# A fixed order for the head of the kernel, a conversion on three engines, and weights from a free place

## Chip, cores, metric

One core of a Trainium2 chip. The metric is the device time of one execution in microseconds (us), lower is better. The engines go by the profile's names: PE is TensorE (matmuls; PEld its weight loads), DVE is VectorE, ACT is ScalarE, POOL is GpSimd, SP is SyncE; ACTq and SPq are the DMA issues of ACT and SP. TensorE is called warm where its matmuls run at full clock and cold where they take about twice as long.

## The reference

```
x   (8, 3008, 256) float32          w_in (256, 2048), w_out (2048, 256) float64
X = real(fft(fft(x, axis=1), axis=2))      # FNet mixing
h = X.reshape(24064, 256) @ w_in
out = maximum(0.01 * h, h) @ w_out
```

The product of a float32 array and a float64 scalar makes both weights float64, so the kernel gets them as pairs of 32-bit words and has to build float32 from them.

## The kernel before

Each sequence is folded, transformed along the sequence by matmuls ("dft"), and the transform along the features is folded into the first weights ("weight fold", `wf`). The body has 384 steps, each an "up" (first product, leaky relu) and, three steps later, a "down" (second product). All of that is one TensorE stream. Feature d=128 has a path of its own: "nyquist", a broadcast `nb`, and weights `wn`. The parts that matter here, cut to their core:

```python
def g_tile():                                     # raw pieces, scratch and the steps' g share 5 buffers
    return work.tile([P, 2 * WN], F32, tag="g", bufs=5, name="raw")

def to_f32(dst, raw, dtype):                      # 512 float64 a partition, all on DVE
    ...
    v.tensor_scalar(man_i, hi, 0xFFFFF, 0x100000, and, or)                          # L240
    v.scalar_tensor_tensor(man, lo * 2.0**-32 + man_i)                              # L241
    v.tensor_scalar(power_i, (hi >> 20) & 0x7FF)                                    # L242
    v.tensor_scalar(power_i, min(max(power_i, 896), 1151))                          # L243
    v.tensor_scalar(power_i, (power_i - 896) * 2**23)                               # L244
    v.scalar_tensor_tensor(power_i, (hi & sign) | power_i)                          # L245
    v.scalar_tensor_tensor(dst, (man * 2.0**-20) * power)                           # L246

def w_in_part(f0):                                # two pieces, tag "win", 2 buffers
    ...
    for w in range(2):                            # weight fold: cosine, sine
        ... matmul(pt, lhsT=feat_sb[:, a, w * P : (w + 1) * P], rhs=win[a]); scalar.copy(wf[...], pt)
    for i in range(4):                            # L265: weights of d=128, one column each
        ... matmul(pt[:, i : i + 1], lhsT=win[a][:, i * P : (i + 1) * P], rhs=feat_sb[:, a, 2 * P : 2 * P + 1])
    nc.scalar.copy(wn[...], pt[:, 0:4])

load_x(0); fold_x(0); load_tab(nc.scalar, ...)    # the scheduler may reorder each engine's work
for f0 in range(0, F, WN): w_in_part(f0)
nyquist(0); dft(units[0], 0); dft(units[0], 1); spread(units[0])
for f in range(0, NH, 2): w_out_part(f)
nyquist(1)
for at in range(len(steps) + lag): up(at); ...; down(at - 3)
```

Of the kernel before, what the change touches and what calls it, by code (L numbers as in the profile page):

```python
# [47 lines left out]
P = 128  # L49
# [10 lines left out]
WN = 512  # L60
SLOPE = 0.01
# [46 lines left out]
def feat_tables():  # L108

    j, d = np.arange(D)[:, None], np.arange(P)[None, :]  # L110
    turn = (j * d) % D
    cos = np.where(4 * turn % (2 * D) == D, 0.0, np.cos(2.0 * np.pi * turn / D))
    sin = np.where(2 * turn % D == 0, 0.0, np.sin(2.0 * np.pi * turn / D))
    nyq = np.where(j % 2 == 0, 1.0, -1.0)
    out = np.zeros((D, 2 * P + 2), np.float32)
    out[:, 0:P] = cos
    out[:, P : 2 * P] = -sin
    out[:, 2 * P :] = nyq
    return out
# [29 lines left out]
def tile_fnet_leaky_relu(  # L149
# [24 lines left out]
    xs = {}  # L174

    def load_x(b):
        t = xp.tile([P, 2, 2, NI * 2, D], F32, tag="x", bufs=1, name="xt")
        for h in range(2):
            nc.sync.dma_start(t[:, h], x[b, :, h].rearrange("p e i r d -> p e (i r) d"))
        xs[b] = t  # L180
# [3 lines left out]
    def fold_x(b):  # L184


        t = xs.pop(b)
        a, z = t[:, :, 0], t[:, :, 1]
        nc.vector.tensor_tensor(a, a, z, op=ALU.add)  # L189
        for h in range(2):  # L190
            lo, hi = a[:, h, :, 1:P], a[:, h, :, P + 1 : D]
            nc.vector.tensor_tensor(z[:, h, :, 1:P], lo, hi, op=ALU.add)
            nc.vector.tensor_tensor(z[:, h, :, P + 1 : D], lo, hi, op=ALU.subtract)
            nc.scalar.copy(z[:, h, :, 0:1], a[:, h, :, 0:1])
            nc.gpsimd.memset(z[:, h, :, P : P + 1], 0.0)
# [5 lines left out]
    feat_sb = const.tile([P, 2, 2 * P + 2], F32, name="feat_sb")  # L201
    nc.sync.dma_start(feat_sb, feat_tab.rearrange("(a p) n -> p a n", p=P))
    load_x(0)
# [4 lines left out]
    nyx = const.tile([P, 2, 2, NI, 2, B], F32, name="nyx")  # L208
    tabs = {}
# [6 lines left out]
    def g_tile():  # L216
        return work.tile([P, 2 * WN], F32, tag="g", bufs=5, name="raw")

    def load_w(src):

        raw = g_tile()
        n = src.shape[1] * src.shape[2]
        dst = raw if src.dtype == F32 else raw.bitcast(src.dtype)
        nc.sync.dma_start(dst[:, 0:n].rearrange("p (c n) -> p c n", c=src.shape[1]), src)
        return raw

    def to_f32(dst, raw, dtype):
# [3 lines left out]
        if dtype == F32:  # L231
            nc.vector.tensor_copy(dst, raw[:, 0:WN])
            return
        hi = raw.bitcast(I32)[:, 0 : 2 * WN].rearrange("p (n w) -> p n w", w=2)[:, :, 1]
        lo = raw.bitcast(U32)[:, 0 : 2 * WN].rearrange("p (n w) -> p n w", w=2)[:, :, 0]
        tmp = g_tile()
        man, power = tmp[:, 0:WN], tmp[:, WN : 2 * WN]
        man_i, power_i = tmp.bitcast(I32)[:, 0:WN], tmp.bitcast(I32)[:, WN : 2 * WN]
        v = nc.vector
        v.tensor_scalar(man_i, in0=hi, scalar1=0xFFFFF, scalar2=0x100000, op0=ALU.bitwise_and, op1=ALU.bitwise_or)  # L240
        v.scalar_tensor_tensor(man, in0=lo, scalar=2.0**-32, in1=man_i, op0=ALU.mult, op1=ALU.add)  # L241
        v.tensor_scalar(power_i, in0=hi, scalar1=20, scalar2=0x7FF, op0=ALU.logical_shift_right, op1=ALU.bitwise_and)  # L242
        v.tensor_scalar(power_i, in0=power_i, scalar1=896.0, scalar2=1151.0, op0=ALU.max, op1=ALU.min)  # L243
        v.tensor_scalar(power_i, in0=power_i, scalar1=-896.0, scalar2=2.0**23, op0=ALU.add, op1=ALU.mult)  # L244
        v.scalar_tensor_tensor(power_i, in0=hi, scalar=-(2**31), in1=power_i, op0=ALU.bitwise_and, op1=ALU.bitwise_or)  # L245
# [206 lines left out]
```

## Time and profile before

| | |
|---|---|
| time, median | 2002.47 us (2002.25 to 2003.03); 2002.72 in the rounds of the change |
| span of the profiled run | 1999.3 us |
| first matmul | 31.29 us |
| TensorE uninterrupted from | 97.47 us |
| one step from then on | 4.66 us |

The prediction below shows the lines. Read them so: TensorE is full from 97 us to the end, so only what happens before that can move the time, and that stretch ("the head") is where DVE is nearly always busy.

### The profile page before, as it was taken

To read this page: it belongs to the slowest core of one execution; us is meant where nothing else is said; L and a number is where in the kernel's file an instruction comes from. 1 tells how busy PE (TensorE), PEld (TensorE's weight loads), DVE (VectorE), ACT (ScalarE), POOL (GpSimd) and SP (SyncE) were. 2 spreads that over 40 slices of the span, in tenths; PEclk is the share of its full clock that TensorE was granted. 3 is DMA by queue.
4 is the path that set the end of the run, shared out by engine and by line. 5 is a ranking of instruction groups with operands and counts; after the bars stand their busy time and mean duration, and the time that the engine had idled before them with its cause. 6 is when DMAs were issued, how large, how long until landed. Compare 5 with 4: busy or idle time off the path is not lost.

```text
span 1999.3 us, 24452 instructions
## 1 busy us (share of the span) xinstructions
PE 1950.6 (98%) x8952; PEld 1691.1 (85%) x8952; DVE 1106.4 (55%) x2111; ACT 439.1 (22%) x496; POOL 1095.0 (55%) x1572
## 2 busy tenths in 40 slices
PE   3799999999999999999999999999999999999999
PEld 1488888888888888888888888888888888888888
DVE  6945654466454744557445475545644475455444
ACT  0122222222222222222222222222222222222221
POOL 0365755566455655556555475555655566455554
PEclk9899999999999999999999999999999999999999
DMA  6301000020000200002000100002000020000000
GB/s 247 101 11 74 19 21 19 11 82 22 11 19 11 92 11 19 11 22 82 11 19 21 74 19 11 29 11 82 14 18 19 11 82 21 11 19 17 16 11 21
DMA packets 23478, 70.98 MB, mean 36 GB/s; under 512 B 2480, under 2 KB 15152, under 8 KB 21312
## 3 DMA queue, kind: packets, MB, share of 16 engines
q1 hardware_dynamic: 22208, 64.80, 8.9%
q10 hardware_dynamic: 1152, 4.63, 0.6%
q8 instruction: 71, 1.16, 0.2%
q14 instruction: 47, 0.39, 0.1%
HBM read 44.71 MB, written 24.71 MB: 35 GB/s over the span
## 4 chain that ended last, share of the span: by engine, by line
PE 96%; DVE 2%; DMA 1%; issue 0%; SPq 0%; DVEq 0%
PE sum_ps L380 57%; PE sin_ps L347 16%; PE cos_ps L347 16%; PE dft_ps L291 6%; PE up_ps L260 1%; DMA xt<-in_x_dram 1%; PE up_ps L265 0%; DVE raw L240 0%; DVE raw L241 0%; DVE raw L245 0%; DVE raw L244 0%; DVE raw L243 0%; DVE xt L189 0%; DVE win L246 0%; DVE wo L246 0%; DVE raw L242 0%
## 5 line engine op out<-in xcount | busy, mean ns | idle before, releaser
L352 DVE SCALAR_TENSOR_TENSOR cos<-nb,wn,cos_ps 128x251 f32<-128x251 f32 (+1 forms) x768 | 330.9, 472 | 731.0 <-PE cos_ps L347 731.0
L362 POOL TENSOR_TENSOR s<-g 128x251 f32<-128x251 f32 (+1 forms) x384 | 294.5, 767 | 783.7 <-ACT g L358 783.7
L358 ACT ACTIVATE g<-g 128x1004 f32<-128x1004 f32 (+1 forms) x384 | 399.1, 1039 | 1347.0 <-DVE g L357 1292.3
L380 PE MATMUL sum_ps<-s,wt 128*128 128x251 f32 (+1 forms) x2304 | 550.3, 374 | 0.0
L380 PEld LDWEIGHTS sum_ps<-s,wt 128*128 128x128 f32 x2304 | 434.2, 188 | 54.5
L347 PE MATMUL sin_ps<-mix,wf 128*128 128x251 f32 (+1 forms) x1536 | 390.6, 376 | 8.7 <-DVE nyq L300 4.8
L347 PE MATMUL cos_ps<-mix,wf 128*128 128x251 f32 (+1 forms) x1536 | 389.7, 376 | 2.0 <-DVE cos L352 2.0
L380 PE MATMUL sum_ps<-g,wo 128*128 128x251 f32 (+1 forms) x1536 | 388.6, 375 | 0.0
L347 PEld LDWEIGHTS sin_ps<-mix,wf 128*128 128x128 f32 x1536 | 291.8, 190 | 44.7 <-DVE nyq L300 5.2
L380 PEld LDWEIGHTS sum_ps<-g,wo 128*128 128x128 f32 x1536 | 291.9, 190 | 40.8
L347 PEld LDWEIGHTS cos_ps<-mix,wf 128*128 128x128 f32 x1536 | 292.3, 190 | 37.2 <-DVE cos L352 2.7
L365 POOL TENSOR_TENSOR s<-g,s 128x251 f32<-128x251 f32 (+1 forms) x384 | 275.1, 716 | 30.1
L363 POOL TENSOR_TENSOR s<-s,g 128x251 f32<-128x251 f32 (+1 forms) x384 | 291.4, 759 | 0.0
L356 DVE TENSOR_TENSOR g<-cos,sin_ps 128x502 f32<-128x502 f32 (+1 forms) x384 | 260.1, 677 | 50.5 <-DVE cos L352 10.5
L357 DVE TENSOR_TENSOR g<-cos,sin_ps 128x502 f32<-128x502 f32 (+1 forms) x384 | 257.4, 670 | 0.0
L364 POOL TENSOR_TENSOR s<-g 128x251 f32<-128x251 f32 (+1 forms) x384 | 253.0, 659 | 0.0
L380 PE MATMUL sum_ps<-s,wo 128*128 128x251 f32 (+1 forms) x768 | 225.2, 375 | 0.0
L380 PE MATMUL sum_ps<-g,wt 128*128 128x251 f32 (+1 forms) x768 | 225.2, 375 | 0.0
L380 PEld LDWEIGHTS sum_ps<-s,wo 128*128 128x128 f32 x768 | 145.6, 190 | 17.0
L380 PEld LDWEIGHTS sum_ps<-g,wt 128*128 128x128 f32 x768 | 145.9, 190 | 16.5
L291 PE MATMUL dft_ps<-tab,xt 128*128 128x377 f32 (+1 forms) x384 | 126.7, 479 | 0.0
L291 PEld LDWEIGHTS dft_ps<-tab,xt 128*128 128x128 f32 x384 | 72.6, 189 | 43.0 <-issue 0.6
(42 smaller groups left out, 434.3 us busy)
## 6 DMA issues: line engine op xcount, KB each, us to landing
xt<-in_x_dram SPq DMA_DIRECT2D x16, 1536.0 KB, 6.5
out_dram<-o SPq DMA_DIRECT2D x80, 251.0 KB, 2.3
tab<-in_seq_tab_dram ACTq DMA_DIRECT2D x8, 565.5 KB, 11.8
raw<-in_w_in_dram SPq DMA_DIRECT2D x8, 512.0 KB, 4.0
raw<-in_w_out_dram SPq DMA_DIRECT2D x8, 512.0 KB, 3.7
out_dram<-o SPq DMA_DIRECT2D x16, 250.0 KB, 2.1
nb<-nyq_dram SPq DMA_DIRECT2D x8, 376.5 KB, 3.5
nb<-nyq_dram SPq DMA_DIRECT2D x8, 376.0 KB
```

What stands on the lines that cost most here:

```text
L260: nc.tensor.matmul(pt, lhsT=feat_sb[:, a, w * P : (w + 1) * P], rhs=win[a], start=(a == 0), stop=(a == 1))
L291: nc.tensor.matmul(ps_t[0:m, 0 : KW[c]], lhsT=z_of(i), rhs=tabs[n, c][:, i, 0 : KW[c]], start=(i == 0), stop=(i == NI - 1))
L347: nc.tensor.matmul(pt[blk][:, h * n : (h + 1) * n], lhsT=wf[:, blk, fs], rhs=mixed[b, c][blk][:, at : at + n], start=True, stop=True)
L352: nc.vector.scalar_tensor_tensor(cos[:, hs], in0=spreads[b, c][:, at : at + n], scalar=wn[:, h * NH + f : h * NH + f + 1], in1=pt[0][:, hs ...
L356: nc.vector.tensor_tensor(g[:, 0], cos[:, 0 : 2 * n], pt[1][:, 0 : 2 * n], op=ALU.add)
L357: nc.vector.tensor_tensor(g[:, 1], cos[:, 0 : 2 * n], pt[1][:, 0 : 2 * n], op=ALU.subtract)
L358: nc.scalar.activation(g, g, ACT.Lrelu)
L362: nc.gpsimd.tensor_tensor(s1, a[1][0], a[1][1], op=ALU.add)
L363: nc.gpsimd.tensor_tensor(s2, s1, a[0][0], op=ALU.subtract)
L364: nc.gpsimd.tensor_tensor(s3, a[0][0], a[1][0], op=ALU.subtract)
L365: nc.gpsimd.tensor_tensor(s4, a[0][1], s2, op=ALU.subtract)
L380: nc.tensor.matmul(sums[j][p], lhsT=still[p], rhs=moving[p], start=(f == 0 and i % 2 == 0), stop=(f == NH - 1), skip_group_check=True)
```

## The change

Its intent: start the TensorE stream earlier by taking float64 work off DVE, taking the one-column matmuls away, and laying the head out by hand. Its core (cuts marked):

```diff
-    out[:, 2 * P :] = nyq
+    out[:, P : P + 1] = nyq          # the sine of d=0 is zero: its column carries d=128's weights
 ...
-        v.tensor_scalar(power_i, ... max 896, min 1151)
-        v.tensor_scalar(power_i, ... -896, * 2**23)
-        v.scalar_tensor_tensor(dst, (man * 2**-20) * power)
+        nc.scalar.activation(man, man_i, ACT.Copy, scale=2.0**-20)
+        nc.scalar.activation(power, power_i, ACT.Relu, scale=-1.0, bias=inf[:, 0:1])
+        nc.scalar.activation(power_i, power, ACT.Relu, scale=-(2.0**23), bias=inf[:, 1:2])
+        nc.gpsimd.tensor_tensor(man, man, power, op=ALU.mult)
 ...
-        ... 16 one-column matmuls a part, scalar.copy(wn)
+        nc.scalar.dma_start(wn_dram row, wf[0:1, 1] ...)      # spread_wn: out and in again through DRAM
+        nc.scalar.dma_start(wn[...], row ...)
 ...
-    raw pieces and scratch in g (5 buffers), win 2 buffers
+    raw pieces in tags o, e, raw (5 buffers), power 2, win 4
 ...
+    with tc.manual_schedule():        # every engine keeps this order
+        w0 = load_w_in(0); t0 = load_x(0, nc.scalar); nc.scalar.dma_start(nyx); feat_sb; w2 = load_w_in(2 * WN)
+        load_tab(nc.scalar, 0..3, 0); o0 = load_w_out(0)
+        w0.begin; w0.end; fold_rows(t0, 0, nc.gpsimd); fold_w_in(0, w0); w1 = load; w2.begin
+        fold_rows(t0, 1, nc.gpsimd); w2.end; fold_halves; fold_nyquist; rest = nyquist(0); fold_w_in(2 * WN, w2)
+        wn_rest = spread_wn(0); o0.begin; rest(); spread; wn_rest(); w3 = load; rest = dft(0); o0.end; combine; rest()
+        rest = dft(1); w1.begin; rest(); step(0); w1.end; fold_w_in(WN, w1); step(1); w3.begin; step(2); w3.end
+        fold_w_in(3 * WN, w3); wn_rest = spread_wn(WN); step(3); o1.begin; wn_rest(); step(4); o1.end; combine; o2.begin
+        step(5); o2.end; combine; o3.begin; step(6); o3.end; combine; load_tab(nc.sync, 0..3, 1); step(7); step(8)
+        nyquist(1)(); spread(units[1])
+    for at in range(9, len(steps) + lag): step(at)
```

`begin` is the part of a conversion up to the activations, `end` what follows them.

More of the change, by code (lines that the diff above doesn't have):

```diff
@@ L60 @@
 WN = 512
+WB = WN // D
 SLOPE = 0.01
@@ L114, in feat_tables @@
     nyq = np.where(j % 2 == 0, 1.0, -1.0)
-    out = np.zeros((D, 2 * P + 2), np.float32)
+    out = np.zeros((D, 2 * P), np.float32)
     out[:, 0:P] = cos
     out[:, P : 2 * P] = -sin
-    out[:, 2 * P :] = nyq
+    out[:, P : P + 1] = nyq
     return out
@@ L172, in dft_ps, with load_x, fold_rows, fold_halves @@
         return up_ps("dft_ps")
-    xs = {}
-    def load_x(b):
+    def load_x(b, q=None):
         t = xp.tile([P, 2, 2, NI * 2, D], F32, tag="x", bufs=1, name="xt")
         for h in range(2):
-            nc.sync.dma_start(t[:, h], x[b, :, h].rearrange("p e i r d -> p e (i r) d"))
-        xs[b] = t
+            (q or nc.sync).dma_start(t[:, h], x[b, :, h].rearrange("p e i r d -> p e (i r) d"))
+        return t
     zs = {}
-    def fold_x(b):
-        t = xs.pop(b)
-        a, z = t[:, :, 0], t[:, :, 1]
-        nc.vector.tensor_tensor(a, a, z, op=ALU.add)
-        for h in range(2):
-            lo, hi = a[:, h, :, 1:P], a[:, h, :, P + 1 : D]
-            nc.vector.tensor_tensor(z[:, h, :, 1:P], lo, hi, op=ALU.add)
-            nc.vector.tensor_tensor(z[:, h, :, P + 1 : D], lo, hi, op=ALU.subtract)
-            nc.scalar.copy(z[:, h, :, 0:1], a[:, h, :, 0:1])
-            nc.gpsimd.memset(z[:, h, :, P : P + 1], 0.0)
+    def fold_rows(t, h, minus):
+        a, z = t[:, h, 0], t[:, h, 1]
+        nc.vector.tensor_tensor(a, a, z, op=ALU.add)
+        lo, hi = a[:, :, 1:P], a[:, :, P + 1 : D]
+        minus.tensor_tensor(z[:, :, P + 1 : D], lo, hi, op=ALU.subtract)
+        nc.vector.tensor_tensor(z[:, :, 1:P], lo, hi, op=ALU.add)
+        nc.scalar.copy(z[:, :, 0:1], a[:, :, 0:1])
+        nc.gpsimd.memset(z[:, :, P : P + 1], 0.0)
+    def fold_halves(b, t):
+        a, z = t[:, :, 0], t[:, :, 1]
         nc.vector.tensor_tensor(a[:, 0], z[:, 0], z[:, 1], op=ALU.add)
@@ L198, in fold_x @@
         zs[b] = a
-    feat_sb = const.tile([P, 2, 2 * P + 2], F32, name="feat_sb")
-    nc.sync.dma_start(feat_sb, feat_tab.rearrange("(a p) n -> p a n", p=P))
-    load_x(0)
+    feat_sb = const.tile([P, 2, 2 * P], F32, name="feat_sb")
     wf = const.tile([P, 2, F], F32, name="wf")
@@ L208, in tile_fnet_leaky_relu @@
     nyx = const.tile([P, 2, 2, NI, 2, B], F32, name="nyx")
+    inf = const.tile([P, 2], F32, name="inf")
+    wn_dram = dram.tile([2, F // 2], F32, name="wn_dram")
     tabs = {}
@@ L214, in load_tab @@
         tabs[n, c] = t
-    def g_tile():
-        return work.tile([P, 2 * WN], F32, tag="g", bufs=5, name="raw")
-    def load_w(src):
-        raw = g_tile()
-        n = src.shape[1] * src.shape[2]
-        dst = raw if src.dtype == F32 else raw.bitcast(src.dtype)
-        nc.sync.dma_start(dst[:, 0:n].rearrange("p (c n) -> p c n", c=src.shape[1]), src)
-        return raw
-    def to_f32(dst, raw, dtype):
-        if dtype == F32:
-            nc.vector.tensor_copy(dst, raw[:, 0:WN])
-            return
-        hi = raw.bitcast(I32)[:, 0 : 2 * WN].rearrange("p (n w) -> p n w", w=2)[:, :, 1]
-        lo = raw.bitcast(U32)[:, 0 : 2 * WN].rearrange("p (n w) -> p n w", w=2)[:, :, 0]
-        tmp = g_tile()
-        man, power = tmp[:, 0:WN], tmp[:, WN : 2 * WN]
-        man_i, power_i = tmp.bitcast(I32)[:, 0:WN], tmp.bitcast(I32)[:, WN : 2 * WN]
-        v = nc.vector
-        v.tensor_scalar(man_i, in0=hi, scalar1=0xFFFFF, scalar2=0x100000, op0=ALU.bitwise_and, op1=ALU.bitwise_or)
-        v.scalar_tensor_tensor(man, in0=lo, scalar=2.0**-32, in1=man_i, op0=ALU.mult, op1=ALU.add)
-        v.tensor_scalar(power_i, in0=hi, scalar1=20, scalar2=0x7FF, op0=ALU.logical_shift_right, op1=ALU.bitwise_and)
-        v.tensor_scalar(power_i, in0=power_i, scalar1=896.0, scalar2=1151.0, op0=ALU.max, op1=ALU.min)
-        v.tensor_scalar(power_i, in0=power_i, scalar1=-896.0, scalar2=2.0**23, op0=ALU.add, op1=ALU.mult)
-        v.scalar_tensor_tensor(power_i, in0=hi, scalar=-(2**31), in1=power_i, op0=ALU.bitwise_and, op1=ALU.bitwise_or)
-        v.scalar_tensor_tensor(dst, in0=man, scalar=2.0**-20, in1=power, op0=ALU.mult, op1=ALU.mult)
@@ L248, in w_in_part, with __init__, word, begin @@
-    def w_in_part(f0):
-        n = w_in.shape[1] // F
-        win = []
-        for a in range(2):
-            raw = load_w(w_in[a * P : (a + 1) * P, n * f0 : n * (f0 + WN)].rearrange("p (c n) -> p c n", c=1))
-            w = work.tile([P, WN], F32, tag="win", bufs=2, name="win")
-            to_f32(w, raw, w_in.dtype)
-            win.append(w)
+    class Weights:
+        def __init__(self, src, dst):
+            n = len(parts)
+            tag, bufs = (("o", 2), ("e", 2), ("raw", 1))[n % 3]
+            self.raw = work.tile([P, 2 * WN], F32, tag=tag, bufs=bufs, name="raw")
+            self.dst = dst
+            self.f64 = src.dtype != F32
+            raw = self.raw if not self.f64 else self.raw.bitcast(src.dtype)
+            nc.sync.dma_start(raw[:, 0 : src.shape[1] * src.shape[2]].rearrange("p (c n) -> p c n", c=src.shape[1]), src)
+            parts.append(self)
+        def word(self, dtype, w):
+            return self.raw.bitcast(dtype).rearrange("p (n w) -> p n w", w=2)[:, :, w]
+        def begin(self):
+            if not self.f64:
+                return
+            hi = self.word(I32, 1)
+            self.power = work.tile([P, WN], F32, tag="power", bufs=2, name="power")
+            man, power = self.dst, self.power
+            man_i, power_i = man.bitcast(I32), power.bitcast(I32)
+            v = nc.vector
+            v.tensor_scalar(man_i, in0=hi, scalar1=0xFFFFF, scalar2=0x100000, op0=ALU.bitwise_and, op1=ALU.bitwise_or)
+            v.tensor_scalar(power_i, in0=hi, scalar1=20, scalar2=0x7FF, op0=ALU.logical_shift_right, op1=ALU.bitwise_and)
+            nc.scalar.activation(man, man_i, ACT.Copy, scale=2.0**-20)
+            nc.scalar.activation(power, power_i, ACT.Relu, scale=-1.0, bias=inf[:, 0:1])
+            nc.scalar.activation(power_i, power, ACT.Relu, scale=-(2.0**23), bias=inf[:, 1:2])
+        def end(self):
+            if not self.f64:
+                nc.vector.tensor_copy(self.dst, self.raw[:, 0:WN])
+                return
+            hi, lo = self.word(I32, 1), self.word(U32, 0)
+            man, power = self.dst, self.power
+            power_i = power.bitcast(I32)
+            v = nc.vector
+            v.scalar_tensor_tensor(man, in0=lo, scalar=2.0**-52, in1=man, op0=ALU.mult, op1=ALU.add)
+            v.scalar_tensor_tensor(power_i, in0=hi, scalar=-(2**31), in1=power_i, op0=ALU.bitwise_and, op1=ALU.bitwise_or)
+            nc.gpsimd.tensor_tensor(man, man, power, op=ALU.mult)
@@ L257, in w_in_part, with load_w_in, fold_w_in @@
+    parts = []
+    def load_w_in(f0):
+        n, made = w_in.shape[1] // F, []
+        for a in range(2):
+            w = work.tile([P, WN], F32, tag="win", bufs=4, name="win")
+            src = w_in[a * P : (a + 1) * P, n * f0 : n * (f0 + WN)].rearrange("p (c n) -> p c n", c=1)
+            made.append(Weights(src, w))
+        return made
+    def fold_w_in(f0, made):
         for w in range(2):
@@ L259, in w_in_part, with spread_wn, rest, load_w_out @@
             for a in range(2):
-                nc.tensor.matmul(pt, lhsT=feat_sb[:, a, w * P : (w + 1) * P], rhs=win[a], start=(a == 0), stop=(a == 1))
+                nc.tensor.matmul(pt, lhsT=feat_sb[:, a, w * P : (w + 1) * P], rhs=made[a].dst, start=(a == 0), stop=(a == 1))
             nc.scalar.copy(wf[:, w, f0 : f0 + WN], pt)
-        pt = up_ps()
-        for i in range(WN // P):
-            for a in range(2):
-                nc.tensor.matmul(pt[:, i : i + 1], lhsT=win[a][:, i * P : (i + 1) * P],
-                                 rhs=feat_sb[:, a, 2 * P : 2 * P + 1], start=(a == 0), stop=(a == 1))
-        nc.scalar.copy(wn[:, f0 // P : f0 // P + WN // P], pt[:, 0 : WN // P])
-    def w_out_part(f):
-        nf = WN // D
+    def spread_wn(f0):
+        row = wn_dram[:, f0 : f0 + WN]
+        nc.scalar.dma_start(row.rearrange("(o h) n -> o h n", o=1), wf[0:1, 1].rearrange("o (h n) -> o h n", h=2)[:, :, f0 : f0 + WN])
+        at = f0 // P
+        def rest():
+            for h in range(2):
+                nc.scalar.dma_start(wn[:, h * NH + at : h * NH + at + WN // P], row[h].rearrange("(q p) -> p q", p=P))
+        return rest
+    def load_w_out(f):
+        made = []
         for h in range(2):
             at = (h * NH + f) * P
-            raw = load_w(w_out[at : at + nf * P, :].rearrange("(c p) d -> p c d", p=P))
-            to_f32(wo[:, h, f : f + nf, :].rearrange("p c d -> p (c d)"), raw, w_out.dtype)
-        b = [[wo[:, h, f : f + nf, i * P : (i + 1) * P] for i in range(2)] for h in range(2)]
-        t = [wt[:, i, f : f + nf, :] for i in range(4)]
+            src = w_out[at : at + WB * P, :].rearrange("(c p) d -> p c d", p=P)
+            made.append(Weights(src, wo[:, h, f : f + WB, :].rearrange("p c d -> p (c d)")))
+        return made
+    def combine_w_out(f):
+        b = [[wo[:, h, f : f + WB, i * P : (i + 1) * P] for i in range(2)] for h in range(2)]
+        t = [wt[:, i, f : f + WB, :] for i in range(4)]
         for to, x, y in ((t[0], b[0][1], b[0][0]), (t[1], b[1][1], t[0]), (t[2], b[1][1], b[0][1]), (t[3], b[1][0], t[1])):
             nc.gpsimd.tensor_tensor(to, x, y, op=ALU.subtract)
-    fold_x(0)
-    for n in range(4):
-        load_tab(nc.scalar, n, 0)
-    for f0 in range(0, F, WN):
-        w_in_part(f0)
-    nc.sync.dma_start(nyx, x_nyq)
     def sequence(ps_t, m, z_of, n, c):
@@ L305, in dft @@
         z = zs[b]
-        t = work.tile([P, UW[0]], F32, tag=f"mix{blk}", bufs=2, name=f"mix{blk}")
         pe, po = dft_ps(), dft_ps()
@@ L309, in dft, with rest, fold_nyquist @@
             sequence(pt, P, lambda i: z[:, (c + blk) % 2, 2 * i + r, blk * P : (blk + 1) * P], 2 * blk + r, c)
-        butterfly(t, pe, po, P, c)
-        mixed.setdefault(u, {})[blk] = t
+        def rest():
+            t = work.tile([P, UW[0]], F32, tag=f"mix{blk}", bufs=2, name=f"mix{blk}")
+            butterfly(t, pe, po, P, c)
+            mixed.setdefault(u, {})[blk] = t
+        return rest
+    nyq_dram = dram.tile([B, 2, UW[0]], F32, name="nyq_dram")
     nya, nyb = nyx[:, :, 0], nyx[:, :, 1]
-    nc.vector.tensor_tensor(nyb, nya, nyb, op=ALU.add)
-    nc.vector.tensor_tensor(nya[:, 0], nyb[:, 0], nyb[:, 1], op=ALU.add)
-    nc.vector.tensor_tensor(nya[:, 1], nyb[:, 0], nyb[:, 1], op=ALU.subtract)
-    nyq_dram = dram.tile([B, 2, UW[0]], F32, name="nyq_dram")
+    def fold_nyquist():
+        nc.vector.tensor_tensor(nyb, nya, nyb, op=ALU.add)
+        nc.vector.tensor_tensor(nya[:, 0], nyb[:, 0], nyb[:, 1], op=ALU.add)
+        nc.vector.tensor_tensor(nya[:, 1], nyb[:, 0], nyb[:, 1], op=ALU.subtract)
     def nyquist(c):
@@ L323, in nyquist, with rest @@
             sequence(pt, B, lambda i: nya[:, c, i, r, :], r, c)
-        t = work.tile([P, UW[0]], F32, tag="mix0", bufs=2, name="nyq")
-        butterfly(t, pe, po, B, c)
-        nc.sync.dma_start(nyq_dram[:, c, 0 : UW[c]], t[0:B, 0 : UW[c]])
+        def rest():
+            t = work.tile([P, UW[0]], F32, tag="mix0", bufs=2, name="nyq")
+            butterfly(t, pe, po, B, c)
+            nc.sync.dma_start(nyq_dram[:, c, 0 : UW[c]], t[0:B, 0 : UW[c]])
+        return rest
     def spread(u):
@@ L384, in down @@
         p1, p2, p3, p4, p5, p6, p7 = (sums[j][p] for p in range(7))
-        o = work.tile([P, 2, 2 * CW], F32, tag="o", bufs=2, name="o")
-        e = work.tile([P, 4, CW], F32, tag="e", bufs=2, name="e")
+        o = work.tile([P, 2 * WN], F32, tag="o", bufs=2, name="o")[:, 0 : 4 * CW].rearrange("p (a n) -> p a n", a=2)
+        e = work.tile([P, 2 * WN], F32, tag="e", bufs=2, name="e")[:, 0 : 4 * CW].rearrange("p (a n) -> p a n", a=4)
         q1, u2, u3, v = (e[:, i, 0:n] for i in range(4))
@@ L393, in down, with step @@
             nc.sync.dma_start(out[d * P : (d + 1) * P, first : first + 2 * n], o[:, d, 0 : 2 * n])
-    nyquist(0)
-    dft(units[0], 0)
-    dft(units[0], 1)
-    spread(units[0])
-    for n in range(4):
-        load_tab(nc.scalar, n, 1)
-    for f in range(0, NH, WN // D):
-        w_out_part(f)
-    nyquist(1)
     lag = 3
-    for at in range(len(steps) + lag):
+    def step(at):
         if at < len(steps):
@@ L411, in tile_fnet_leaky_relu @@
             if n + 1 < len(units) and f == 4:
+                if part == 0 and n > 0:
+                    spread(units[n + 1])
                 if part == 0:
-                    spread(units[n + 1])
                     if c == 1:
-                        fold_x(b + 1)
+                        t = xs.pop(b + 1)
+                        for h in range(2):
+                            fold_rows(t, h, nc.vector)
+                        fold_halves(b + 1, t)
                 else:
-                    dft(units[n + 1], part - 1)
+                    dft(units[n + 1], part - 1)()
@@ L418, in tile_fnet_leaky_relu @@
             if c == 0 and part == 2 and f == 6 and b + 1 < B:
-                load_x(b + 1)
+                xs[b + 1] = load_x(b + 1)
         if at >= lag:
             down(*steps[at - lag])
+    xs = {}
+    with tc.manual_schedule():
+        nc.vector.memset(inf[:, 0:1], 1151.0)
+        nc.vector.memset(inf[:, 1:2], 255.0 * 2.0**23)
+        w0 = load_w_in(0)
+        t0 = load_x(0, nc.scalar)
+        nc.scalar.dma_start(nyx, x_nyq)
+        nc.sync.dma_start(feat_sb, feat_tab.rearrange("(a p) n -> p a n", p=P))
+        w2 = load_w_in(2 * WN)
+        for n in range(4):
+            load_tab(nc.scalar, n, 0)
+        o0 = load_w_out(0)[:]
+        for w in w0:
+            w.begin()
+        for w in w0:
+            w.end()
+        fold_rows(t0, 0, nc.gpsimd)
+        fold_w_in(0, w0)
+        w1 = load_w_in(WN)
+        for w in w2:
+            w.begin()
+        fold_rows(t0, 1, nc.gpsimd)
+        for w in w2:
+            w.end()
+        fold_halves(0, t0)
+        fold_nyquist()
+        rest = nyquist(0)
+        fold_w_in(2 * WN, w2)
+        wn_rest = spread_wn(0)
+        for w in o0:
+            w.begin()
+        rest()
+        spread(units[0])
+        wn_rest()
+        w3 = load_w_in(3 * WN)
+        rest = dft(units[0], 0)
+        for w in o0:
+            w.end()
+        combine_w_out(0)
+        o1 = load_w_out(WB)
+        rest()
+        rest = dft(units[0], 1)
+        for w in w1:
+            w.begin()
+        rest()
+        step(0)
+        for w in w1:
+            w.end()
+        fold_w_in(WN, w1)
+        step(1)
+        for w in w3:
+            w.begin()
+        step(2)
+        for w in w3:
+            w.end()
+        fold_w_in(3 * WN, w3)
+        wn_rest = spread_wn(WN)
+        o2 = load_w_out(2 * WB)
+        step(3)
+        for w in o1:
+            w.begin()
+        wn_rest()
+        step(4)
+        for w in o1:
+            w.end()
+        combine_w_out(WB)
+        o3 = load_w_out(3 * WB)
+        for w in o2:
+            w.begin()
+        step(5)
+        for w in o2:
+            w.end()
+        combine_w_out(2 * WB)
+        for w in o3:
+            w.begin()
+        step(6)
+        for w in o3:
+            w.end()
+        combine_w_out(3 * WB)
+        for n in range(4):
+            load_tab(nc.sync, n, 1)
+        step(7)
+        step(8)
+        nyquist(1)()
+        spread(units[1])
@@ L424 @@
+    for at in range(9, len(steps) + lag):
+        step(at)
 def kernel(x, moe_w_in, moe_w_out):
```

## The prediction

> **What bounds the kernel now.** I read the page first: busy shares, then the 40 slices.
>
> ```profile
> PE 1950.6 (98%) x8952; PEld 1691.1 (85%) x8952; DVE 1106.4 (55%) x2111; ACT 439.1 (22%) x496; POOL 1095.0 (55%) x1572
> PE   3799999999999999999999999999999999999999
> DVE  6945654466454744557445475545644475455444
> PEclk9899999999999999999999999999999999999999
> PE 96%; DVE 2%; DMA 1%; issue 0%; SPq 0%; DVEq 0%
> ```
>
> TensorE (PE) is full from the third slice (about 100 us) to the end, and 96% of the chain that ended last is PE. The body is a PE stream that no other engine holds up; only the first 100 us, the head, have slack. The matmuls of the body are untouched by the change, so the question is only when the stream starts. I then read the busy times by stretch and the PE timeline of the head.
>
> ```profile
> 16.00:40.00 24.00, 7.75 (x25) 4.00 (x25) 22.20 (x37) 2.90 (x6) 0.33 (x2) 1.00 0.57 217
> 40.00:63.00 23.00, 21.69 (x84) 11.79 (x84) 20.26 (x40) 4.46 (x10) 1.10 (x1) 0.93 0.44 138
> 63.00:97.40 34.40, 23.76 (x69) 14.19 (x69) 34.13 (x67) 4.77 (x6) 14.09 (x18) 0.75 0.33 100
> ```
>
> ```profile
> 31.29 2.08 PE L260 MATMUL up_ps<-win,feat_sb 128*128 128x512 f32 x2 [31.29 <-DVE win L246]
> 76.59 1.01 PE L347 MATMUL cos_ps<-mix,wf 128*128 128x251 f32 x4
> 82.37 2.04 PE L347 MATMUL sin_ps<-mix,wf 128*128 128x251 f32 x4 [4.77 <-DVE nyq L300]
> 86.37 2.04 PE L347 MATMUL cos_ps<-mix,wf 128*128 128x251 f32 x4 [1.96 <-DVE cos L352]
> 92.32 2.01 PE L347 MATMUL sin_ps<-mix,wf 128*128 128x251 f32 x4 [3.91 <-DVE g L357]
> 97.47 1.06 PE L380 MATMUL sum_ps<-g,wo 128*128 128x251 f32 x4
> ```
>
> Columns of the first: stretch, length, then busy us of PE, weight load, DVE, ACT (ScalarE), POOL (GpSimd), PE clock, DMA share, GB/s. From 16 us, when x has landed, to 97.4 us DVE is busy 76.6 of 81.4 us (22.20 + 20.26 + 34.13); ACT has 12, POOL 15.5. So the head is **DVE-bound**: it converts 16 float64 pieces, seven instructions each. PE starts at 31.29 us, waits on DVE in gaps of 4.77, 1.96 and 3.91 us, and from 82 us runs at half clock (2.04 us for what takes 1.01). The stream proper starts at 97.47 us with the first "down" (L380); there four "up" steps are done, and a step costs 4.66 us from then on (8 matmul records of "up" at 0.212 us, 1.69 us; 14 of "down", 2.97 us).
>
> The yardstick: the end of the eleventh "down" with fourteen "ups" done, leaving out the sequence transform that falls there. Before: 97.47 + 10 x 4.665 + 2.97 = 147.1 us. All later work is the same in both kernels, so the change moves the time by what it moves this mark.
>
> **What the Trainium skill says.** (1) "ScalarE: Activation LUTs", section "What ACT_TABLE_LOAD costs": an activation takes 186 ns + 0.833 ns per element, 93 ns more with a bias read per partition, and neighbours overlap by 93 ns; 512 elements give 613 and 706 ns. The trace agrees: the 128x512 copy takes 585 ns. (2) "TensorE: Matmul & The Clock Gate", section "What's actually happening": after an idle window of about 3.4 us PE runs at half clock until about 3.4 us of sustained work. The trace agrees: 2.04 against 1.01 us after the 4.77 us gap. (3) "DMA: Bandwidth & Descriptors", section "Issuing engines are not separate DMA queues": issuing from several engines gives no extra bandwidth. The trace agrees: DMA sits near 410 GB/s to 24 us, with x, tables and weights sharing it, and x lands at 16.2 us. (4) "GPSIMD Engine Reference", section "Specifications": its SBUF interface is shared with VectorE. The trace agrees: a 128x256 POOL subtraction takes 0.73 to 1.10 us and DVE's first conversion instruction 0.42 alone, up to 0.95 beside POOL.
>
> **The change part by part.** Durations are from these groups and lines:
>
> ```profile
> L245 DVE SCALAR_TENSOR_TENSOR raw<-raw 128x512 int32<-128x512 int32 x16 | 11.5, 718 | 0.2
> L244 DVE TENSOR_SCALAR raw<-raw 128x512 int32<-128x512 int32 x16 | 7.5, 468 | 0.2
> L265 PE MATMUL up_ps<-feat_sb,win 128*128 128x1 f32 x64 | 7.6, 244 | 0.0
> L279 POOL TENSOR_TENSOR wt<-wo 128x256 f32<-128x256 f32 x8 | 7.2, 894 | 48.0 <-DVE wo L246 48.0
> 0.73 15.21 ACTq L213 DMA_DIRECT2D tab<-in_seq_tab_dram  x8
> 15.97 1.28 ACT L194 ACT_TABLE_LOAD   x1 [15.97 <-DMA tab<-in_seq_tab_dram]
> ```
>
> *Conversion.* Before: 4 TENSOR_SCALAR at 0.335 us start to start and 3 SCALAR_TENSOR_TENSOR at 0.60 = 3.14 us of DVE a piece, 50 us in all. After: 2 + 2 = 1.87 us, 30 us in all: **20 us leave DVE**. Added: ACT three activations a piece (0.53 + 0.61 + 0.61 = 1.75 us, 28 us), POOL one 512-wide multiply (251 wide takes 0.72, so an estimate of 1.45 us; 23 us). Throughput would allow a much earlier stream. But a piece becomes a chain through three engines: DVE 0.7, ACT 1.75, DVE 1.2, POOL 1.45.
>
> *d=128 weights.* 64 one-column matmuls go, 7.6 us of PE in a time when DVE was the bound, so worth little by themselves. A write to DRAM and two reads come in; with the 1.7 us that the write of nyq takes before its reader is issued, an estimate of 4 to 5 us before the first step and again before step 4.
>
> *Fixed order.* Each engine now runs the head in program order. Walking through it, each start the latest of the engine's previous end and its inputs:
>
> ACT issues x, nyx and four tables first. In the trace the same ACT queue stood 15.21 us over eight issues, each later one until an older transfer had landed (the ninth issue of both queues came when the first had landed, 5.46 against 0.73 + 4.7). So I take ACT to be held until x has landed, about 16 to 17 us, then 1.28 us of table load. The first piece landed at 5 us, but its ACT part starts at 18.8; DVE, in order behind it, cannot fold x meanwhile (it did so at 16.3 before). First pieces done 24.7; first weight fold on a cold PE (8 x 0.43, the first 4.5 us doubled, 6.0) 30.7. ACT copies, second pieces (ACT 31.3 to 34.9), fold of x 39.0, nyquist 39.5 to 45.7, second fold 49.2, ACT on the w_out piece 50 to 54, then the nyq copy, which frees PSUM for dft: 54.3 to 60.6, second dft 64.6, its copy behind two more ACT pieces, mix ready 67.1, **first step's g at 69.3** (before: 92.1). So far 23 us are gained.
>
> From there it is lost again. Step 0 takes POOL to 73.1, only then the multiplies of w1 (76.0), fold on a cold PE 82.1, ups 1 and 2 85.5; w3 the same way: POOL behind step 2 until 96.4, cold fold 102.4, up 3 and down 0 107.1; wn for step 4 lands 113; the pieces of o1 are multiplied on POOL behind step 4, down 2 waits until 125; steady from there, with the second nyquist (4.0): mark at **171.5**, that is +24 us.
>
> Parts of this are soft. With PE never cold the same walk gives 156.9; with ACT free at 8 us and PE warm, 147.7; with POOL 20% slower, 175.8. The walk is likely pessimistic: warm-up may be shorter, and instructions of steps 9 and on, outside the fixed region, may fill PE's waits (two or three ups, 3 to 5 us). And an order with so many split halves was probably tried out against the clock. I therefore take a shift of about +2 us, well below the walk.
>
> **The rivals.** (A) *DVE relief counts in full*: the head shortens by the 20 us of conversion and some of the PE gaps: 1970 to 1985 us. For it: DVE is 94% busy in the head. Against: the in-order ACT and POOL queues, and PE, once idle, is cold. A floor: the PE work to the mark is 32 folds' matmuls 13.7, nyquist 7.9, dft 7.9, 14 ups 23.7, 11 downs 32.7 = 86 us, after a first fold that can hardly begin before 14: 100 to 111, so even a perfect order gains 36 to 47 us; over 2% (40 us) needs nearly that. (B) *The serial chain eats the gain*: the walk in full, 2010 to 2027. For it: the ACT queue's hold in the trace, and three engines in series. (C) *An ACT table switch at each change between Relu and Lrelu*: 1.28 us each, some 10 more; the skill's same page says cheap functions are in every set, and the trace has just two loads. I give it little. (D) *The body suffers* because POOL or buffers changed: its PE row is full and no body instruction changes; nothing.
>
> **Range and chances.** Centre 2002.5 + 2 = 2004 us. Low end: half to two thirds of the largest gain, 1978. High end: the walk plus slow POOL, 2028. Faster by over 2% needs a mark under 107, close to the floor: 0.05. Slower by over 2% needs 187, beyond the walk's worst: 0.03. The rest, 0.92.
>
> **What would show it.** Right: DVE's conversion records fall from 112 to 64, ACT gets 48, POOL 16; no L265 group; PE full after some 110 to 130 us with the same 4.66 us step; ACT's first activation not before 15 us; first g near 69 us; PE gaps before the second and fourth weight folds, put down to the POOL multiply, with matmuls at half clock after them. Wrong: if ACT starts near 8 us and the first fold near 14, rival A holds; if PE is full by 100 us with "up" steps of batch positions beyond 9 in the head, hoisting filled the gaps; if PE gaps appear after 150 us, the body was touched after all.

## The result

2025.93 us (2024.82 to 2027.16) against 2002.72 us before; ratio 1.0116, 95% interval 1.0099 to 1.0134. A ratio is the mean time of one kernel's fast runs over that of the other's fast runs of the same rounds, so not quite the ratio of the medians quoted. The change makes the kernel 1.2% slower. All outputs are right. The range of the prediction held it; its centre was 22 us low.

The page after, the lines that answer to those of before:

```profile
PE 1950.9 (96%) x8888; PEld 1684.3 (83%) x8888; DVE 1100.7 (54%) x2071; ACT 470.4 (23%) x540; POOL 1121.8 (55%) x1590
PE   2589999999999999999999999999999999999999
PEclk8789999999999999999999999999999999999999
PE 94%; ACT 1%; DVE 1%; POOL 1%; DMA 1%; issue 0%; ACTq 0%; SPq 0%; DVEq 0%; POOLq 0%
```

The body is as full as before; the second and third slices have become emptier (5 and 8 tenths against 7 and 9), and the clock is lower in them. TensorE's busy time is the same 1951 us in a span 23.9 us longer, though 64 matmul records are gone, which fits the lower clock.

Busy time by stretch after (stretch, length, then us of PE, weight load, DVE, ACT, POOL, clock, DMA share, GB/s):

```profile
16.00:40.00 24.00, 7.56 (x8) 2.35 (x8) 17.69 (x17) 10.28 (x17) 12.22 (x8) 0.93 0.38 145
40.00:63.00 23.00, 16.68 (x40) 7.11 (x41) 9.32 (x17) 5.80 (x10) 3.59 (x2) 0.80 0.15 47
63.00:97.40 34.40, 13.89 (x37) 7.72 (x35) 18.33 (x31) 13.46 (x19) 17.35 (x21) 0.70 0.27 83
```

DVE is busy 45 of 81 us (17.69 + 9.32 + 18.33) where it was busy 76.6. It was relieved, but no other engine took over as the bound: from 63 to 97 us all four are at about half load or less (DVE 53%). They wait for each other. The TensorE timeline shows where:

```profile
24.34 2.08 PE L280 MATMUL up_ps<-win,feat_sb 128*128 128x512 f32 x2 [24.34 <-POOL win L263]
43.98 5.30 PE L313 MATMUL dft_ps<-tab,nyx 128*8 128x377 f32 x12 [10.82 <-DVE nyx L345]
49.21 3.70 PE L280 MATMUL up_ps<-win,feat_sb 128*128 128x512 f32 x8
78.24 6.67 PE L280 MATMUL up_ps<-win,feat_sb 128*128 128x512 f32 x8 [7.41 <-POOL win L263]
98.26 5.20 PE L280 MATMUL up_ps<-win,feat_sb 128*128 128x512 f32 x8 [9.97 <-POOL win L263]
104.99 1.01 PE L411 MATMUL sum_ps<-g,wo 128*128 128x251 f32 x4
121.50 2.43 PE L411 MATMUL sum_ps<-g,wo 128*128 128x251 f32 x4 [7.02 <-POOL wo L263]
128.73 1.01 PE L378 MATMUL cos_ps<-mix,wf 128*128 128x251 f32 x4
```

The first fold starts 7 us earlier than before, but then TensorE stands 10.82, 7.41, 9.97 and 7.02 us, and the folds after a wait take 6.67 and 5.20 us for work that takes 3.70 us warm (the fold at 49.21 us). It runs without such gaps from 128.73 us, where the kernel before does from 97.47 us (with more work left then).

ScalarE's queue after, and DVE and POOL at the conversion (group: count, busy us, mean ns, then idle before and its releaser):

```profile
9.14 9.37 ACTq L215 DMA_DIRECT2D tab<-in_seq_tab_dram  x4
18.54 1.28 ACT L249 ACT_TABLE_LOAD   x1 [18.54 <-DMA raw<-in_w_in_dram]
```

```profile
L262 DVE SCALAR_TENSOR_TENSOR power<-raw,power 128x512 int32<-128x512 int32 x16 | 14.2, 890 | 1.4 <-ACT power L251 1.4
L263 POOL TENSOR_TENSOR win<-win,power 128x512 f32<-128x512 f32 x8 | 13.7, 1720 | 24.6 <-DVE power L262 24.6
L248 DVE TENSOR_SCALAR power<-raw 128x512 int32<-128x512 int32 x16 | 11.5, 717 | 4.8 <-POOL wo L263 4.8
```

ScalarE is held by its own DMA issues until 18.5 us. The records of the conversion on DVE fall from 112 to 64, but their busy time only from 63.6 to 49.4 us. The four instructions a piece that stayed took 38.3 us before; they took 11 us more now, because a record got longer (L262 890 ns; its like before, L245, 718).

### The profile page after: what moved, and what is told of

Same layout as the page of the kernel before. It is cut to its first block, busy times and chain, and to the rows that moved or that the text cites. A ratio compares the mean times of both kernels' runs of the same rounds, so it can differ in the third digit from the quotient of the medians.

```text
span 2023.2 us, 24341 instructions
## 1 busy us (share of the span) xinstructions
PE 1950.9 (96%) x8888; PEld 1684.3 (83%) x8888; DVE 1100.7 (54%) x2071; ACT 470.4 (23%) x540; POOL 1121.8 (55%) x1590
## 4 chain that ended last, share of the span: by engine, by line
PE 94%; ACT 1%; DVE 1%; POOL 1%; DMA 1%; issue 0%; ACTq 0%; SPq 0%; DVEq 0%; POOLq 0%
PE sum_ps L411 56%; PE cos_ps L378 16%; PE sin_ps L378 16%; PE dft_ps L313 6%; PE up_ps L280 1%; DMA raw<-in_w_in_dram 1%; ACT power L250 0%; POOL win L263 0%; ACT power L251 0%; ACT g L389 0%; POOL s L393 0%; DVE cos L383 0%; POOL s L394 0%; DVE power L248 0%; POOL wo L263 0%
## 6 DMA issues: line engine op xcount, KB each, us to landing
xt<-in_x_dram ACTq DMA_DIRECT2D x2, 1536.0 KB, 12.4
```

## The experiments

Two theories. **F**: the fixed order loses; each engine stands in order behind waits for the others. **C**: the shared conversion itself loses (its chain through three engines, POOL and DVE beside each other). The twelve runs, each a median with its ratio to the kernel before:

| run | what | us | ratio |
|---|---|---|---|
| (change) | | 2025.93 | 1.0116 |
| e1_auto | change, free order | 1985.18 | 0.992 |
| e2_conv | before + shared conversion | 2003.59 | 1.0011 |
| e3_sine | before + sine place | 1994.49 | 0.9967 |
| e4_both | before + both | 2007.27 | 1.003 |
| e5_act | change, ScalarE not held | 2019.1 | 1.0087 |
| e6_early | change, w1 and w3 ahead of step 0 | 2013.0 | 1.0056 |
| e7_warm | change, filler matmuls | 2023.83 | 1.0111 |
| e8_autoact | e1 + ScalarE not held | 1982.91 | 0.9907 |
| e9_bufs | e4 + buffers of its own | 1992.37 | 0.9955 |
| e10_nopool | e8 + multiply and x fold on DVE | 1976.54 | 0.9876 |
| e11_warm2 | e7, filler mended | 2020.88 | 1.0099 |
| e12_fixmul | change, multiply on DVE | 2023.7 | 1.0114 |

### e1_auto: the fixed order lifted

```diff
-    with tc.manual_schedule():
+    if True:
```

> The changed kernel with the fixed order lifted: the head is emitted in the same program order, but each engine may take instructions in another order. Theory F (the fixed order is what loses: engines stand in order behind waits): most of the 24 us comes back and more, 1975 to 2000 us, first gaps before the weight folds gone. Rival C (the conversion shared by three engines loses by its own chain and by POOL and DVE sharing SBUF): stays at 2015 us or above.

Measured: 1985.18 us, ratio 0.992 (0.9905 to 0.9934). Against the change's 1.0116 that is 2%, or 41 us of medians, from one line. TensorE's first wait and first "down" of this run:

```profile
29.00 2.08 PE L280 MATMUL up_ps<-win,feat_sb 128*128 128x512 f32 x2 [29.00 <-POOL win L263]
72.66 1.01 PE L411 MATMUL sum_ps<-g,wo 128*128 128x251 f32 x4
```

The first fold is later than in the change (29.00 against 24.34 us), yet the first "down" comes at 72.66 us against 104.99. So it is what stands between them that the fixed order stretched. F holds for this order: the same instructions in a free order beat the kernel before by 0.8%. (That every fixed order would lose is not shown; e6_early below is a better one.)

### e2_conv, e3_sine, e4_both: the parts alone in the kernel before

e2 puts the shared conversion into `to_f32` (scratch still in g); e3 the sine place:

```diff
 e2:
-        v.tensor_scalar(...) L243, L244; v.scalar_tensor_tensor(dst, ...) L246
+        three activations; nc.gpsimd.tensor_tensor(dst, man, power, op=ALU.mult)
 e3:
-        pt = up_ps(); 16 one-column matmuls; nc.scalar.copy(wn[...], pt[:, 0:4])
+    nc.sync.dma_start(wn_dram, wf[0:1, 1])
+    nc.sync.dma_start(wn, wn_dram[0].rearrange("(q p) -> p q", p=P))     # once, after the four parts
```

> The kernel before with the shared conversion alone (free order, old weights for d=128). Theory F: DVE loses some 20 us of work in a head where it was busy 94%, so 10 to 20 us faster, 1982 to 1992 us. Rival C: no faster, 2002 us or slower, with the gaps before the weight folds put down to POOL.

> The kernel before with the d=128 weights from the sine place alone (one trip through DRAM for all of them). 64 one-column matmuls fall away (7.6 us of PE busy) in a head that waits on DVE; the trip through DRAM lies beside that. Both theories: within 4 us of before, 1997 to 2004 us.

> The kernel before with shared conversion and sine place, free order. Theory F: the two gains add, now that PE and the wn copies matter a little more: 1975 to 1990 us. Rival C: 2000 us or slower.

Measured: e2 2003.59 us, no gain (1.0011, 0.9997 to 1.0026), where F expected 10 to 20 us. e3 1994.49 us, 8 us faster by the medians and 7 by the ratio, more than either theory expected. Before, DVE waited for the one-column matmuls (L265) to release `win`:

```profile
DVE win L246 <- PE up_ps L265: 2.8, 3, 1.4
```

In e3 it does not, and from 16 to 63 us DVE is busy 46.2 us (23.85 + 22.30) against 42.5 (22.20 + 20.26). The rest of the gain was not traced. e4 2007.27 us, slower than before, so the gains do not add. By these runs C looks right for this buffer layout. The POOL timeline of e4_both shows why; each multiply waits for its own piece or, in the first line, for a `win` buffer that a fold still reads:

```profile
35.62 1.29 POOL L250 TENSOR_TENSOR win<-raw 128x512 f32<-128x512 f32 x1 [2.69 <-PE up_ps L264]
39.60 1.29 POOL L250 TENSOR_TENSOR win<-raw 128x512 f32<-128x512 f32 x1 [2.68 <-DVE raw L249]
44.20 1.29 POOL L250 TENSOR_TENSOR win<-raw 128x512 f32<-128x512 f32 x1 [3.32 <-DVE raw L249]
```

One piece comes out each 4.0 to 4.6 us: the conversion runs one piece at a time, a chain of DVE, ScalarE, DVE and POOL, with no second piece beside it. And POOL slows DVE: an instruction of 0.42 us that starts beside the multiply at 35.62 takes 1.49 us and ends 0.3 us after it (37.19 against 36.91),

```profile
35.70 1.49 DVE L244 TENSOR_SCALAR raw<-raw 128x512 int32<-128x512 int32 x1
```

Why e4 is 4 us slower than e2 by the medians (the intervals overlap) although the sine place gains 7 to 8 us alone was not settled.

### e9_bufs: e4 with buffers of its own

```diff
-        raw = g_tile()
+        raw = work.tile([P, 2 * WN], F32, tag=("o", "e", "raw")[n % 3], bufs=(2, 2, 1)[n % 3], name="raw")
-        tmp = g_tile(); man, power = tmp[:, 0:WN], tmp[:, WN : 2 * WN]
+        man = dst; power = work.tile([P, WN], F32, tag="power", bufs=2, name="power")
-        win bufs=2
+        win bufs=4
```

> Run e4_both (2007 us: the kernel before with shared conversion and sine place, free order) with the raw pieces and the exponent in buffers of their own, as the changed kernel has them, instead of in the five shared g buffers, and four win buffers for two. If the buffers make the shared conversion run one piece at a time there (one piece each 4.0 to 4.6 us in e4_both), this frees it: 1982 to 1992 us, near e1_auto. Rival (the order of emission, weights first and x on the other queue, is what helped e1_auto): 2000 us or more.

Measured: 1992.37 us (0.9955, 0.9941 to 0.997), at the edge of the expected range and 15 us better than e4_both. The multiplies of this run, on POOL:

```profile
35.78 1.38 POOL L254 TENSOR_TENSOR win<-win,power 128x512 f32<-128x512 f32 x1 [1.80 <-DVE power L253]
38.30 1.65 POOL L254 TENSOR_TENSOR win<-win,power 128x512 f32<-128x512 f32 x1 [1.14 <-DVE power L253]
41.34 1.29 POOL L254 TENSOR_TENSOR win<-win,power 128x512 f32<-128x512 f32 x1 [1.39 <-DVE power L253]
```

A piece comes each 2.5 to 3.0 us here (some later ones 4.2). So the buffers are what made e4 lose; 7 us remain to e1_auto, which also has another order of emission and x on the other queue. C is wrong as a general verdict: with these buffers the shared conversion costs nothing that these runs can see. That it gains is not shown by this run: e9 holds the sine place too, and e3, with the sine place alone, is only 2 us behind (1994.49; its interval, 0.995 to 0.9983, overlaps that of e9).

### e5_act and e8_autoact: ScalarE not held by DMA issues

```diff
-        nc.scalar.dma_start(nyx, x_nyq)
+        nc.sync.dma_start(nyx, x_nyq)
-            load_tab(nc.scalar, n, 0)
+            load_tab(nc.sync, n, 0)
```

> The changed kernel, fixed order kept, with nyx and the four tables issued from the SP queue, so that ScalarE is no longer held to 18.5 us by its own DMA issues. Walk of the prediction with ScalarE free at once: the mark comes 8 us earlier, so 2017 to 2021 us against 2026. Rival: the x fold and later waits (POOL behind the steps) absorb the earlier start, 2023 us or more.

> The free order (run e1_auto, 1985 us) with nyx and tables issued from the SP queue: ScalarE starts near 9 us instead of 23.2 us. If the start of the conversion sets the free order's head, 1974 to 1981 us. Rival (x fold and DVE set it): within 4 us of 1985.

Measured: e5 2019.1 us (1.0087), e8 1982.91 us (0.9907). The first activation and the first fold of e5_act:

```profile
8.34 0.63 ACT L249 ACTIVATE win<-win 128x512 f32<-128x512 int32 x1 [5.39 <-DVE win L247]
16.61 2.08 PE L280 MATMUL up_ps<-win,feat_sb 128*128 128x512 f32 x2 [16.61 <-POOL win L263]
```

The activation starts when the first piece has landed, and the first fold 7.7 us earlier than in the change; 7 us of it reach the end in the fixed order (6 by the ratios, whose intervals just overlap), near the 8 of the walk. In the free order only some 2 us do, within the intervals of e1 and e8 (0.9905 to 0.9934 and 0.9892 to 0.9922): the rival held there.

### e6_early: w1 and w3 converted ahead of step 0

```diff
+        for w in w1: w.end()
+        for w in w3: w.begin()
+        fold_w_in(WN, w1)
+        for w in w3: w.end()
+        fold_w_in(3 * WN, w3)
         step(0)
-        w1.end; fold_w_in(WN, w1)
         step(1)
-        w3.begin
         step(2)
-        w3.end; fold_w_in(3 * WN, w3)
```

> The changed kernel, fixed order kept, but the pieces w1 and w3 are converted and folded ahead of step 0 instead of between steps 0 to 3. If the stand of TensorE behind POOL's multiplies, which are emitted behind a step's POOL work, is what loses, the walk gives 15 us: 2008 to 2015 us, the gaps of 7.4 and 10.0 us before the weight folds gone. Rival (the gaps only move to another place): 2022 us or more.

Measured: 2013.0 us (1.0056), 13 us better than the change.

```profile
73.70 7.39 PE L280 MATMUL up_ps<-win,feat_sb 128*128 128x512 f32 x10 [9.90 <-POOL win L263]
81.92 2.84 PE L280 MATMUL up_ps<-win,feat_sb 128*128 128x512 f32 x6 [0.83 <-POOL win L263]
```

One wait of 9.90 us is left of the two of 7.41 and 9.97, where the expectation had both gone. The two folds now follow each other, so the wait and the slow clock are paid once. In size it is near what the walk said, 13 of 15 us. If the gains of e5 and e6 add, which was not run, they make some 20 of the 41 us of e1_auto; the rest is not assigned to single waits.

### e7_warm and e11_warm2: keeping the clock up

```diff
+    def warm(n, tag="sum"):           # n matmuls 128x256 whose result nobody reads
+        t = ps.tile([P, 512], F32, tag=tag, bufs=4, name="warm")
+        for _ in range(n): nc.tensor.matmul(t[:, 0:256], lhsT=feat_sb[:, 0, 0:P], rhs=feat_sb[:, 0, 0:256], start=True, stop=True)
+    # in the waits of TensorE: ahead of nyquist(0), of dft(1), after step(0), after step(2), ahead of down 2
```

> The changed kernel with idle-time filler: 68 matmuls of no use in TensorE's waits (before nyquist 14, before the second dft 4, after step 0 16, after step 2 20, before down 2 14), each shorter than the wait it fills, so that the clock stays full. If the half clock after waits costs what the trace shows (nyquist 5.30 against 3.96, folds 6.67 and 5.20 against 3.5, down 2 6.6 against 3.0, dft 5.76 against 3.96: 11.6 us in sum), 2011 to 2018 us. Rival (the waits are set by the other engines, so a faster TensorE only waits longer): 2022 us or more.

> Run e7_warm with the filler mended: in e7_warm the filler before nyquist ended 5 us early (TensorE was cold again) and that after step 0 ran 3.3 us over. Now 24, 5, 7, 22, 16 matmuls. If the half clock costs what the walk says, 2010 to 2018 us; if the other engines' waits take up what TensorE saves, 2021 us or more, as e7_warm.

Measured: e7 2023.83 us, where the filler missed two of its five places (it ended 5 us too early before nyquist and ran over after step 0), so that run tells little. e11, mended: 2020.88 us (1.0099, 1.0082 to 1.0116), 5 us better than the change by the medians, 3 by the ratios, whose intervals still overlap; that is between the two expectations. The nyquist and the fourth fold of e11_warm2:

```profile
43.45 3.97 PE L318 MATMUL dft_ps<-tab,nyx 128*8 128x377 f32 x12 [0.95 <-DVE nyx L350]
94.61 4.06 PE L285 MATMUL up_ps<-win,feat_sb 128*128 128x512 f32 x8 [0.48 <-POOL win L263]
```

They run at full clock (3.97 for 5.30 us, 4.06 for 5.20 us), and still "down 2" waits for POOL's pieces and starts its second pair of records only at 117.97 us. This agrees with the Trainium skill, "TensorE: Matmul & The Clock Gate", section "What's actually happening", on the half clock after idle time: folds of 6.67 and 5.20 us after waits of 7.41 and 9.97 us, 4.06 us each with the waits filled. The half clock costs some 3 to 5 us where the filler reached it. That is no test of the whole 14.6 that the walk gives for a TensorE that is never cold: the four pieces of work that became warm lasted 6.8 us longer in the change (22.93 against 16.17 us), while the first fold, the end of "down 2" and the "up" after a 5.59 us wait stayed cold here too.

### e12_fixmul: the multiply on DVE in the fixed order

```diff
-            nc.gpsimd.tensor_tensor(man, man, power, op=ALU.mult)
+            v.tensor_tensor(man, man, power, op=ALU.mult)
```

> The changed kernel, fixed order kept, with the last multiply of the conversion on DVE instead of POOL. If the weight folds wait for a multiply that stands behind a step's POOL work, the walk gives 9 us: 2014 to 2019 us, waits of TensorE before the second and fourth weight folds 2 to 3 us shorter each. Rival (ScalarE's part of the chain comes later anyway): 2023 us or more.

Measured: 2023.7 us (1.0114), 2 us better at most. The number is the rival's.

```profile
75.62 2.04 PE L280 MATMUL up_ps<-win,feat_sb 128*128 128x512 f32 x2 [3.86 <-DVE win L263]
78.80 5.12 PE L280 MATMUL up_ps<-win,feat_sb 128*128 128x512 f32 x6 [1.14 <-DVE win L263]
```

The fold starts earlier but waits again at once for the second piece, whose DVE instructions are stretched by the step's POOL work beside them (in this trace the multiply on DVE takes 0.69 us alone and 1.09 to 1.17 us there); most of the fold is where it was (78.80 against 78.24 us). The run does get ahead later: the work after "down 2" starts at 124.35 us against 128.73 in the change. But TensorE then waits for DVE, which has the multiplies now, ahead of the second nyquist, a wait that the change does not have:

```profile
141.03 3.96 PE L313 MATMUL dft_ps<-tab,nyx 128*8 128x376 f32 x12 [1.81 <-DVE cos L383]
```

So the multiply on POOL is worth little by itself: a releaser's name is not yet the cause. That the order of the pieces and steps is, e6_early supports.

### e10_nopool: a version that beats both

```diff
 (e8_autoact, and)
-            nc.gpsimd.tensor_tensor(man, man, power, op=ALU.mult)
+            v.tensor_tensor(man, man, power, op=ALU.mult)
-        fold_rows(t0, 0, nc.gpsimd); fold_rows(t0, 1, nc.gpsimd)
+        fold_rows(t0, 0, nc.vector); fold_rows(t0, 1, nc.vector)
```

> Run e8_autoact (1983 us) with the last multiply of the conversion and one part of the x fold on DVE instead of POOL. In e8_autoact the chain from 66 to 95 us is POOL, and DVE instructions of 0.42 and 0.95 us stretch to 1.5 and 2.5 us beside POOL's. If POOL is the bound of that head, 1970 to 1979 us. Rival (DVE, loaded with 11 us more, becomes the bound again): 1983 us or more.

The first "down" of e8_autoact and of this run:

```profile
70.23 1.01 PE L411 MATMUL sum_ps<-g,wo 128*128 128x251 f32 x4
54.81 1.01 PE L411 MATMUL sum_ps<-g,wo 128*128 128x251 f32 x4
```

Measured: 1976.54 us (0.9876, 0.9861 to 0.9891): 1.2% faster than before and, by the two ratios, 2.4% faster than the change. In the free order, where the chain from 66 to 95 us was POOL, taking POOL's share away helps by 6 us, though DVE gets the work back. (Of the 15 us at the first "down", later waits take most; which of the two edits gains was not separated.)

## Why the prediction was right, and where not

**The walk was right.** Its steps stand beside the measured ones:

| | walk | trace after |
|---|---|---|
| first weight fold starts | 24.7 | 24.34 |
| x folded, nyquist starts | 39.5 | 43.98 |
| second dft done | 64.6 | 64.66 |
| g of step 0 done | 69.3 | 72.2 |
| fold of w1 starts | 76.0 | 78.24 |
| fold of w3 starts | 96.4 | 98.26 |
| down 0 done | 107.1 | 107.96 |
| wn for step 4 there (DVE's first use) | 113 | 113.06 |
| down 2 starts | 125 | 121.50 |
| mark | 171.5 | 170.8 |

("Done" is read as the start of the next matmul. The mark after: the eleventh "down" starts at 171.61, takes 2.97, less 3.79 for the dft that falls before it.) Walk +24 us, measured mark +23.7 us, span +23.9 us, medians +23.2 us. The gain up to step 0 and its loss in the steps after it came as told: first g at 72.2 us, 20 us ahead of before, then given back. The signs that it named came too: 64, 48 and 16 records on DVE, ACT and POOL, no one-column matmuls, ACT's first activation at 19.84 us, and gaps before two folds put down to POOL's multiply, with slow matmuls after them.

That the end agrees within 1 us is partly luck. "Down 2" started 3.5 us earlier than told, but from there to the mark it took 49.3 us and not 46.5: "steady from there" left out that "down 2" itself runs cold, with a short wait in it (7.2 us for 2.97). x was folded 4.5 us later than told, which cost nothing because the first dft, told for 54.3 us, could start at 52.75.

**The step that failed is the last one**, "I therefore take a shift of about +2 us, well below the walk". Its three grounds, checked:
- "instructions of steps 9 and on ... may fill PE's waits": none did. Up to down 2 at 121.50 us TensorE ran just six "ups", those of steps 0 to 5, in order.
- "warm-up may be shorter": with five of its waits filled (e11_warm2) the kernel gains 3 to 5 us, and the walk itself has 14.6 for no cold TensorE at all, so the clock could not carry 22.
- "an order with so many split halves was probably tried out against the clock": a guess about people, not about the chip. It was wrong: one line (e1_auto) takes the order away and gains 41 us.

**Terms mis-sized inside the walk.** "20 us leave DVE" (counted from start to start): in busy time 25 us left, but 11 came back as records beside POOL grew (63.6 to 49.4). The 512-wide multiply on POOL, estimated at 1.45 us: 1.72 us mean for win, 1.41 for wo (1.24 us alone at 76.93 us, 2.71 at 24.91 us beside DVE's two-input work). "64 one-column matmuls ... worth little by themselves": 7 to 8 us in e3_sine; 2.8 of it is the wait of DVE, the bound, for the two `win` buffers that they held. ScalarE held "until x has landed, about 16 to 17 us": until 18.5, when x had long landed (1.2 + 12.4 us), and the profile names a weight piece on the other queue as the releaser. The high end, "the walk plus slow POOL, 2028", is not its own sum: 2002.5 + 175.8 - 147.1 is 2031.

**Rivals.** A (DVE relief counts in full, 1970 to 1985 us) was wrong for the change. With the order free, e1, e8 and e10 land at 1985 to 1977, its range, but its mechanism is not shown by that: the sine place is part of it, and e10, the fastest, gives work back to DVE. B (serial chain, 2010 to 2027) held. C (table switches): two table loads in the head, as expected, none more. D (body): the step stays 4.66 us.

## What to carry to other kernels

A fixed order binds every engine to the waits of its neighbours. Before fixing one, walk it through with measured durations, engine by engine, and do not discount the result by guesses; here a relieved engine gained nothing because no other work could pass the one it waited for. Spreading a chain over more engines lost here while the buffers held one item at a time (e4) and stopped losing when a second could run beside the first (e9); that it pays by itself, these runs do not show.

## What the Trainium skill lacked or had wrong

- "DMA: Bandwidth & Descriptors", section "Issuing engines are not separate DMA queues", weighs only the time to issue and calls it usually small beside the transfer. What it lacks: in this kernel an engine that computes and issues was held by its issues. ScalarE's last four alone took from 9.14 to 18.51 us (change). It did its first activation at 19.8 us in the change, at 8.3 us with five issues moved to SP (e5_act), worth 6 to 7 us.
- On DVE and POOL slowing each other and on the half clock after waits, the runs show nothing that the skill lacks.
